# Storing gK and gV from ScalarE's queue, two steps late, in the stage that runs the second pass alone

## The chip, the cores and the metric

The kernel runs on one core of one Trainium2 chip. A core has five engines that each work through a queue of their own in order: TensorE (PE; its weight loads are shown as PEld), VectorE (DVE), ScalarE (ACT), GpSimd (POOL) and SyncE (SP). All share 16 DMA engines, to which SP, ACT and POOL can issue transfers. The metric is the time of one execution on the device in microseconds; the kernel before takes 891.21 us (median of 3 runs, 891.13 to 893.05).

## What is computed

The reference is one decoder layer in decode (2 batches, one token, width 640, 32 heads of 128, a cache of 4096 positions for each head, a two-layer MLP), and its gradients for seven inputs:

```python
q = (x @ wq).reshape(B, Sq, Hq, Dh) ...
scores = jnp.einsum("bhqd,bhkd->bhqk", q, k) * (Dh ** -0.5)
p = _softmax(scores, axis=-1)
o = jnp.einsum("bhqk,bhkd->bhqd", p, v)
...
h = x + _A_ref(_layernorm(x, axis=-1), A_k_cache, A_v_cache, A_wq, A_wo)
h2 = h + _B_ref(_layernorm(h, axis=-1), B_w1, B_w2)
...
_out, _vjp = jax.vjp(_f, A_x, A_k_cache, A_v_cache, A_wq, A_wo, B_w1, B_w2)
```

Nearly all bytes belong to the caches. K and V are read (64 tiles of 1 MB each, one for each batch and head), and their gradients gK and gV are written (again 64 tiles of 1 MB each). For one head, with one query row, both gradients are outer products: gV is the softmax column times a row of the output's gradient, gK is the gradient of the scores times the row q.

## The kernel before

**Two passes.** The first pass (`p1_iter`, one call for a head) reads K and V and computes the scores, the softmax weights P, the attention's output and what the projections need. The second pass (`p2_iter(j)`, one call for a head) needs the gradient of the attention's output, which is known once the layer has been run forward and back as far as there. It reads V again (tile Wt; the last six heads of each batch were kept on the chip), and writes gK and gV. `plan` (lines 1157 to 1168) lists the iterations: first pass alone, then a stage where every second iteration of the first pass is joined by one of the second, then the second pass alone, which begins at its iteration 14 of 64 and at about 470 us. The change touches this last stage.

**One iteration of the second pass** is a generator with six steps; the main loop (lines 1267 to 1274) runs one step, then whatever load is due (`pump`), then a bit of the background work: the weight gradients (TensorE's o_ps, line 980, ScalarE's casts to ot, line 986, and their stores from ScalarE's queue, line 989), the gradient of x (VectorE's gxj at line 678) and the output projections' gradients. In iteration j:

- Four groups of transposes of Wt on TensorE (line 424, into two PSUM banks t_ps), each copied by ScalarE to t_sb (line 429) and then multiplied with the gradient row into dp (line 437).
- At the head of the iteration the last product of the iteration before is finished (`last_dp`), and VectorE makes the score gradient gsp from it (line 858). The broadcast of two rows for j goes through PSUM (line 877) into rb, by ScalarE (line 882); GpSimd makes pp, a copy of P (line 884).
- VectorE makes gK of iteration j - 1 in two halves (line 844), the first at the head, the second in step 2. At the end of step 2 it is stored (line 899) and its buffer given back.
- VectorE makes gV of iteration j in two halves, in steps 5 and 6. Up to iteration 32 of this stage the last eight of its 32 blocks are made by ScalarE (line 930). At the end of step 6 it is stored (line 931) and its buffer given back.

**What sets the order.** The order of the instructions on each engine is the order in which the program writes them; the engines meet by semaphores that are placed for every tile. Buffers of 1 MB are handed out by `take` and `give`, which keep lists by purpose: "ld" for loads, "g" for gK and gV, "f" for ot, "q" for weights. A buffer that was given back can be taken at once in the program; on the chip its next writer then waits until the store has landed. In the stage with the second pass alone "g" begins with five buffers and gets more as other tiles fall free (lines 1227 to 1238). All loads are issued from SP's queue (line 445 for K, V and W, line 1066 for wqs), the stores of gK and gV from GpSimd's (lines 899, 909, 931, 941), those of ot from ScalarE's.

The functions that the change touches:

Of the kernel before, what the change touches and what calls it, by code (L numbers as in the profile page):

```python
# [15 lines left out]
def kernel(  # L16
# [20 lines left out]
    nc = tc.nc  # L37
# [402 lines left out]
    def natural(cache, b, h):  # L440
        return cache[b, h].rearrange("(p sc) d -> p sc d", sc=NSC)
# [412 lines left out]
    def score_grad(j, c):  # L854
# [5 lines left out]
            in1=P_bf[:, b * H + h, :, None].to_broadcast([128, NSC, 2]), op0=ALU.add, op1=ALU.mult)  # L860
        return gsp

    def p2_iter(j, busy, act=0, own_gK=False, early=False):

        c = S2[j] if j < NP1 else None
        p = S2.get(j - 1)
        if p is not None:
            bp, hp = turns[j - 1]
            last_dp(j - 1, p)
            gsp = score_grad(j - 1, p)  # L870
        if c is not None:
            b, h = turns[j]
            go = gom[:, h, b, :, :]

            bank = pst([128, 512], FP32, "sps", "dp_ps")
            for k, col in enumerate((goc, qsc)):
                nc.tensor.matmul(bank[:, 128 + k * 128:256 + k * 128],  # L877
                                 lhsT=col[:, h, b:b + 1].to_broadcast([128, 128]), rhs=ident_bf[:],
                                 start=True, stop=True)
            c["dp"] = bank[:, 0:NSC]  # L880
            rb = mats.tile([128, 256], BF16, tag="rb", bufs=3, name="rb")
            nc.scalar.activation(out=rb[:], in_=bank[:, 128:384], func=ACT.Copy, scale=rt[:, b, h:h + 1])  # L882
            pp = small.tile([128, NSC, 2], BF16, tag="pp", bufs=2, name="pp")
            nc.gpsimd.tensor_copy(out=pp[:], in_=P_bf[:, b * H + h, :, None].to_broadcast([128, NSC, 2]))
            c.update(rb=rb, pp=pp)
            if act:
                pa = small.tile([128, 8], FP32, tag="pa", bufs=2, name="pa")
                nc.gpsimd.tensor_copy(out=pa[:], in_=P_bf[:, b * H + h, NSC - act:NSC])
            c["T0"] = pair_transpose(c["W"], 0, busy=busy)
        if p is not None:  # L890
            gK = take("g", [128, NSC, 128], "gK")
            outer_half(gK, p["rb"][:, 128:256], gsp, 0)
        yield
        if early:
            gV = take("g", [128, NSC, 128], "gV")
            outer_half(gV, c["rb"][:, 0:128], c["pp"], 0)
        if p is not None:
            outer_half(gK, p["rb"][:, 128:256], gsp, 1)
            nc.gpsimd.dma_start(out=natural(out_2, bp, hp), in_=gK[:])  # L899
            give(gK)  # L900
            del S2[j - 1]
        yield
        if c is None:
            return
        c["T1"] = pair_transpose(c["W"], 1, busy=busy)
        pair_matvec(c["dp"], c.pop("T0"), 0, go)
        if early:
            outer_half(gV, c["rb"][:, 0:128], c["pp"], 1)
            nc.gpsimd.dma_start(out=natural(out_3, b, h), in_=gV[:])
        yield  # L910
        c["T2"] = pair_transpose(c["W"], 2, busy=busy)
        pair_matvec(c["dp"], c.pop("T1"), 1, go)
        yield
        c["T3"] = pair_transpose(c["W"], 3, busy=busy)
        give(c["W"], "g" if j < H and j != 1 and owned["g"] < 3 else None)
        pair_matvec(c["dp"], c.pop("T2"), 2, go)
        if early:
            give(gV)
            yield
            last_dp(j, c)  # L920
            gsp = score_grad(j, c)
        else:
            gV = take("g", [128, NSC, 128], "gV")
            outer_half(gV, c["rb"][:, 0:128], c["pp"], 0)
            yield
            if own_gK:
                last_dp(j, c)
            outer_half(gV, c["rb"][:, 0:128], c["pp"], 1, act)
            for k in range(act):
                nc.scalar.activation(out=gV[:, NSC - act + k, :], in_=c["rb"][:, 0:128], func=ACT.Copy, scale=pa[:, k:k + 1])  # L930
            nc.gpsimd.dma_start(out=natural(out_3, b, h), in_=gV[:])  # L931
            give(gV)
            if own_gK:
                gsp = score_grad(j, c)
            yield
        if own_gK:
            gK = take("g", [128, NSC, 128], "gK")
            outer_half(gK, c["rb"][:, 128:256], gsp, 0)
            yield
            outer_half(gK, c["rb"][:, 128:256], gsp, 1)  # L940
            nc.gpsimd.dma_start(out=natural(out_2, b, h), in_=gK[:])
            give(gK)
            del S2[j]
            yield

# [267 lines left out]
    def p2_step():  # L1213
        nonlocal g2
        try:
            next(g2)
        except StopIteration:
            g2 = None

    for n, (i, j) in enumerate(plan):  # L1220
        all_go = all(("go", B - 1, h) in done for h in range(H))
        if i is None and plan[n - 1][0] is not None:
            pkp.release()
            big1 = tc.alloc_tile_pool(name="big1", bufs=1)
            for _ in range(2):
                more_home("ld", big1)
            share(ld=KEPT[1] + 4, g=5)
        if all_go and not late[0]:
            wop.release()
            big3 = tc.alloc_tile_pool(name="big3", bufs=1, side="right")  # L1230
            for tag in ("ld", "g", "g", "q", "q", "q"):
                more_home(tag, big3)
        late[0] = all_go
        more = int(late[0])
        if fin is not None and not bg2 and not bg3:
            share(ld=8 + 3 * more, g=7 + 3 * more)
        elif fin is not None and j >= H + KEPT[1] - 1:
            share(ld=5 + more, g=6 + 2 * more, f=3, q=2 + 3 * more)
        if j is not None:
            while g2 is not None:  # L1240
                p2_step()
            if j < NP1:
                bg_until(("go", *turns[j]))
            g2 = p2_iter(j, 0, 8 if i is None and j <= H else 0, i is not None and plan[n + 1][1] is None, j < EARLY)
        if i is None and ("w1", 1) in done and fin is None:
            wts.release()
            fin = tc.alloc_tile_pool(name="fin", bufs=1)
            big2 = tc.alloc_tile_pool(name="big2", bufs=1)
            more_home("f", big2)
            banks.update(sps=[2, 3], o=[4, 5, 6])  # L1250
            bg2.append(("fin", fin_gen(fin)))
            bg3.append(("gx", gx_gen(fin)))
        if i == 12:
            bg.append(("ga", ga_gen()))
        if i == H + 2:
            banks["bc"].insert(0, banks["sps"].pop(0))
        elif i == P2_AT:
            banks["bc"].remove(7)
            banks["sps"].insert(0, banks["bc"][0])
            banks["bc"] = [7]  # L1260
        rate = RATES[0 if i is not None and i <= H + 1 else 1 if j is None and i < P2_AT else
                     2 if i is not None else 3 if j <= H else 4]
        if i is None:
            spread[0] = 2
            at_k[0] = 1
            k = 0
            while g2 is not None:
                p2_step()
                pump()
                slot[0] = int(k in ((1, 3, 5) if j <= H else (1, 4)))  # L1270
                k += 1
                bg_step(0, rate)
                bg_step(1, RATE2 * (0.4 if spreading[0] else 1.0))
                bg_step(2, RATE3)
            continue
        at = MIXED if j is not None else REST
        for k, _ in enumerate(p1_iter(i, i < H + 1, 0)):
            for _ in range(at.get(k, 0)):
                if g2 is not None:
                    p2_step()  # L1280
            if k == 5 and not H + 2 < i < P2_AT + 6:
                a_heads(i)
            pump()

            spread[0] = 1 if i < P2_AT else 2
            at_k[0] = k
            if i >= P2_AT:
                slot[0] = int(k == 6 or (k == 1 and j is not None))
            elif i > H + 1:
                slot[0] = {1: 2, 3: 1, 4: 1, 6: 1}.get(k, 0)  # L1290
            else:
                slot[0] = int(k in (1, 6))
            bg_step(0, rate)
            bg_step(1, 0.0)
        if i is not None and i in (H + 1, NP1 + 1):
            bg.append((f"m{i // H - 1}", middle_gen(i // H - 1)))
    forced[0] = True
    slot[0] = 99
    left = [q for q in (bg, bg3, bg2) if q]
# [38 lines left out]
```

## Time and profile before

| what | value |
|---|---|
| runs | 891.21 us median (891.13 to 893.05) |
| the profiled execution | 888.48 us, with a span of 886.3 us |
| busy in the span | PE 738.8 us, PEld 618.2, DVE 681.3, ACT 498.8, POOL 204.1 |
| DMA | 361.85 MB, 408 GB/s over the span |
| loads and SP's stores (q1) | 211.13 MB, 57.8% of the 16 engines' time |
| GpSimd's stores (q0) | 134.23 MB, 36.5% |
| ScalarE's stores (q10) | 14.92 MB, 4.1% |
| from issue to landing, median | gV 14.9 us, gK 15.0, Wt 11.6 |
| the chain that ended last | PE 35%, DMA 34%, DVE 16%, ACT 7%, issue 5% |

The profile is taken from one execution. Its span runs from the first to the last instruction of the program; 2.2 us of the execution lie around it. "Busy" counts instructions that compute; issues of DMAs count on GpSimd alone. The DMA share is the mean busy share of the 16 engines, which take packets from all queues. A wait is shown with what ended it: "DVE gV L844 <- DMA out_dram<-gK" is VectorE's operation at line 844 that writes gV, which waited until a store of gK had landed.

### The profile page before, as it was taken

How to read it: one execution, taken by the hardware profiler on the slowest of the kernel's cores; microseconds unless marked ns; L12 is line 12 of the kernel's file. 1: busy time of each engine (PE TensorE's matmuls, PEld its weight loads, DVE VectorE, ACT ScalarE, POOL GpSimd, SP SyncE). 2: the span in 40 equal slices, each digit the busy share in tenths (PEclk: the TensorE clock that was granted, in tenths of full speed). 3: DMA queues.
4: the chain of work that ended last, by engine and by line, in shares of the span. 5: the costliest groups of instructions: out<-in, count | busy, mean ns of one | idle time of the engine just before them, and what ended most of it. 6: DMA issues, size and time to landing. Idle time of an engine off the chain costs nothing.

```text
span 886.3 us, 24732 instructions
## 1 busy us (share of the span) xinstructions
PE 738.8 (83%) x10143; PEld 618.2 (70%) x10143; DVE 681.3 (77%) x1281; ACT 498.8 (56%) x1292; POOL 204.1 (23%) x358
## 2 busy tenths in 40 slices
PE   4999899999999997988868767787877899867690
PEld 4887788888887886877757656665656667564550
DVE  2666787877788896876778887878788689989861
ACT  1444343446776664654536767777656766545570
POOL 1344433343312010000011332222222111111220
PEclk9999999999999999998995655555566755555555
DMA  9999999999879999999999999999999999999996
GB/s 380 423 420 414 417 409 417 425 423 412 332 295 402 423 423 426 422 426 425 414 398 396 418 421 421 420 413 420 419 416 403 417 425 420 425 425 425 425 424 275
DMA packets 56289, 361.85 MB, mean 408 GB/s; under 512 B 5680, under 2 KB 11760, under 8 KB 15472
## 3 DMA queue, kind: packets, MB, share of 16 engines
q1 hardware_dynamic: 34520, 211.13, 57.8%
q0 software_dynamic: 18432, 134.23, 36.5%
q10 hardware_dynamic: 3224, 14.92, 4.1%
q8 instruction: 80, 1.31, 0.5%
q14 instruction: 33, 0.27, 0.1%
HBM read 211.11 MB, written 149.13 MB: 406 GB/s over the span
## 4 chain that ended last, share of the span: by engine, by line
PE 35%; DMA 34%; DVE 16%; ACT 7%; issue 5%; SPq 0%; POOL 0%; ACTq 0%; POOLq 0%; DVEq 0%
DMA Vt<-in_A_v_cache_dram 15%; PE t_ps L424 14%; DMA out_dram<-gK 11%; PE m_ps L460 9%; DVE gK L844 4%; DVE gV L844 4%; DMA out_dram<-gV 3%; ACT gV L930 3%; PE s_ps L437 3%; DMA wqs<-in_A_wq_dram 3%; DVE pk L470 2%; PE u_ps L498 2%; ACT t_sb L429 2%; PE dp_ps L437 2%; DVE gxj L678 2%
## 5 line engine op out<-in xcount | busy, mean ns | idle before, releaser
L429 ACT COPY t_sb<-t_ps 128x512 f32<-128x512 f32 x479 | 273.1, 587 | 192.4 <-PE t_ps L424 188.6
L437 PEld LDWEIGHTS <-t_sb 128*128 128x128 bf16 x4096 | 178.9, 102 | 63.8 <-ACT t_sb L429 36.2
L424 PE MATMUL t_ps<-ident_f,Wt 128*128 128x128 f32 x832 | 198.6, 389 | 0.9 <-ACT t_sb L429 0.9
L470 DVE TENSOR_TENSOR pk<-Kt,ep 128x2048 bf16<-128x2048 bf16 (+1 forms) x128 | 152.6, 1193 | 47.1 <-ACT ep L524 29.0
L460 PE MATMUL m_ps<-pk,Vt 128*128 128x129 bf16 x2048 | 172.0, 223 | 19.9 <-DMA Vt<-in_A_v_cache_dram 18.8
L844 DVE TENSOR_TENSOR gK<-rb,gsp 128x2048 bf16<-128x2048 bf16 x128 | 153.4, 1227 | 13.3 <-DMA out_dram<-gV 8.5
L460 PEld LDWEIGHTS <-Vt 128*128 128x128 bf16 x2048 | 125.6, 99 | 50.2 <-issue 28.4
L424 PEld LDWEIGHTS t_ps<-ident_f,Wt 128*128 128x128 f32 x832 | 138.2, 202 | 31.9 <-issue 25.2
L424 PE MATMUL t_ps<-ident_f,Kt 128*128 128x128 f32 x1024 | 156.0, 286 | 2.5 <-DMA Kt<-in_A_k_cache_dram 1.9
L844 DVE TENSOR_TENSOR gV<-rb,pp 128x2048 bf16<-128x2048 bf16 (+1 forms) x128 | 142.7, 1139 | 16.3 <-DMA out_dram<-gK 9.9
L486 POOL COPY pk<-ep 128x16 bf16<-128x16 bf16 x80 | 83.6, 1046 | 158.4 <-ACT ep L524 80.0
L424 PEld LDWEIGHTS t_ps<-ident_f,Kt 128*128 128x128 f32 x1024 | 113.9, 145 | 5.0 <-ACT t_sb L429 2.7
L437 PE MATMUL dp_ps<-gom,t_sb 128*128 128x2 bf16 x2048 | 96.0, 168 | 25.1 <-ACT t_sb L429 24.7
L931 POOL DMA_DIRECT2D out_dram<-gV x62 | 33.0, 533 | 305.3 <-DVE gsp L858 135.1
L437 PE MATMUL s_ps<-qm,t_sb 128*128 128x2 bf16 x2048 | 87.4, 164 | 1.5 <-DVE t_sb L427 1.5
L986 ACT CAST ot<-o_ps 128x512 bf16<-128x512 f32 (+3 forms) x152 | 67.5, 491 | 8.4 <-DMA out_dram<-ot 5.2
L588 ACT CAST MT<-m_ps 128x128 bf16<-128x128 f32 x64 | 17.0, 266 | 94.5 <-PE m_ps L460 94.4
L899 POOL DMA_DIRECT2D out_dram<-gK x53 | 28.2, 533 | 135.4 <-DVE gK L844 104.9
L882 ACT ACTIVATE rb<-dp_ps,rt 128x256 bf16<-128x256 f32 x64 | 30.2, 472 | 44.7 <-PE dp_ps L877 43.4
L678 DVE CUSTOM_DVE_ANT_0 hbc<-wo_t,hbc 128x640 bf16<-128x640 bf16 x64 | 52.8, 825 | 0.3
L678 DVE CUSTOM_DVE_ANT_0 gxj<-wqs,gqr 128x1024 bf16<-128x1024 bf16 x40 | 48.7, 1217 | 1.0 <-DMA wqs<-in_A_wq_dram 0.8
L930 ACT ACTIVATE gV<-rb,pa 128x128 bf16<-128x128 bf16 x152 | 46.5, 392 | 3.9 <-DMA out_dram<-gK 3.9
(205 smaller groups left out, 758.2 us busy)
## 6 DMA issues: line engine op xcount, KB each, us to landing
Kt<-in_A_k_cache_dram SPq DMA_DIRECT2D x64, 1024.0 KB, 19.4
Vt<-in_A_v_cache_dram SPq DMA_DIRECT2D x64, 1024.0 KB, 15.5
out_dram<-gV POOLq DMA_DIRECT2D x64, 1024.0 KB, 14.9
out_dram<-gK POOLq DMA_DIRECT2D x64, 1024.0 KB, 15.0
Wt<-in_A_v_cache_dram SPq DMA_DIRECT2D x52, 1024.0 KB, 11.6
wq_t<-in_A_wq_dram SPq DMA_DIRECT2D x5, 1024.0 KB, 7.8
wo_t<-in_A_wo_dram SPq DMA_DIRECT2D x4, 1280.0 KB, 17.6
wqs<-in_A_wq_dram SPq DMA_DIRECT2D x5, 1024.0 KB, 22.3
```

Of the source, the lines that this page charges most:

```text
L424: nc.tensor.transpose(t_ps[:, j, :], natf[:, 2 * cc:2 * cc + 2, :].rearrange("p c k -> p (c k)"), ident_f[:])
L429: nc.scalar.copy(out=t_sb[:], in_=t_ps[:])
L437: nc.tensor.matmul(dst[:, sc:sc + 2], lhsT=v[:, j, :, par], rhs=vecs[:, par, :], start=(par == 0), stop=(par == 1))
L460: nc.tensor.matmul(r["m"][:, 0:129], lhsT=r["V"][:, sc, :], rhs=r["pk"][sc // HALF][:, sc % HALF, 0:129], start=(sc == 0), stop=(sc == NSC ...
L470: nc.vector.tensor_tensor(out=p["pk"][k][:, 0:n, 0:128].rearrange("p s (a two) -> p s a two", two=2), in0=p["K"][:, sl, :].rearrange("p s ...
L486: nc.gpsimd.tensor_copy(out=col, in_=e)
L678: nc.vector.tensor_tensor_reduce(out=junk[0:kc, 0:width], in0=in0, in1=in1, scale=1.0, scalar=0.0, op0=ALU.mult, op1=ALU.add, accum_out=acc)
L844: nc.vector.tensor_tensor(out=pairs_view(dst[:, sl, :]), in0=row.rearrange("p (a two) -> p a two", two=2)[:, None, :, :].to_broadcast([128 ...
L882: nc.scalar.activation(out=rb[:], in_=bank[:, 128:384], func=ACT.Copy, scale=rt[:, b, h:h + 1])
L930: nc.scalar.activation(out=gV[:, NSC - act + k, :], in_=c["rb"][:, 0:128], func=ACT.Copy, scale=pa[:, k:k + 1])
L931: nc.gpsimd.dma_start(out=natural(out_3, b, h), in_=gV[:])
L986: nc.scalar.copy(out=ot[0:P, k, n0:n0 + nn], in_=o_ps[0:P, 0:nn])
```

## The change

Two helpers, `store` and `send`, take the place of the four stores and of the `give` calls behind them. Before the stage in which the second pass runs alone, `store` does as before: it issues from GpSimd and gives the buffer back. In that stage it only notes the tile. `send` is called after every step of the second pass; a noted tile is stored from ScalarE's queue, and its buffer given back, in the second step after the one that completed it. What is left after the last iteration is sent at once.

```diff
+    unsent = []
+    alone = [False]
+    LAG = 2
+
+    def store(out_ap, t):
+
+        if alone[0]:
+            unsent.append([LAG, out_ap, t])
+        else:
+            nc.gpsimd.dma_start(out=out_ap, in_=t[:])
+            give(t)
+
+    def send(all_of_them=False):
+
+        for entry in list(unsent):
+            entry[0] -= 1
+            if entry[0] < 0 or all_of_them:
+                nc.scalar.dma_start(out=entry[1], in_=entry[2][:])
+                give(entry[2])
+                unsent.remove(entry)
+
...
             outer_half(gK, p["rb"][:, 128:256], gsp, 1)
-            nc.gpsimd.dma_start(out=natural(out_2, bp, hp), in_=gK[:])
-            give(gK)
+            store(natural(out_2, bp, hp), gK)
...
-            nc.gpsimd.dma_start(out=natural(out_3, b, h), in_=gV[:])
-            give(gV)
+            store(natural(out_3, b, h), gV)
...
         except StopIteration:
             g2 = None
+        send()
...
         if i is None:
+            alone[0] = True
             spread[0] = 2
...
+    send(True)
     forced[0] = True
```

The stores at lines 909 and 941 are changed in the same way. On ScalarE the store of gV then stands behind the first of the four transpose copies of the next iteration, and the store of gK behind the third.

More of the change, by code (lines that the diff above doesn't have):

```diff
@@ L930, in p2_iter @@
                 nc.scalar.activation(out=gV[:, NSC - act + k, :], in_=c["rb"][:, 0:128], func=ACT.Copy, scale=pa[:, k:k + 1])
-            nc.gpsimd.dma_start(out=natural(out_3, b, h), in_=gV[:])
-            give(gV)
+            store(natural(out_3, b, h), gV)
             if own_gK:
@@ L940, in p2_iter @@
             outer_half(gK, c["rb"][:, 128:256], gsp, 1)
-            nc.gpsimd.dma_start(out=natural(out_2, b, h), in_=gK[:])
-            give(gK)
+            store(natural(out_2, b, h), gK)
             del S2[j]
```

## The prediction

> **What bounds the kernel now.** I read, in this order: the page's DMA parts (2, 3, 6), a table of windows over the stage in which only the second pass runs (about 470 to 870 us), the waits, and the timeline at two places of that stage and at the end.
>
> ```profile
> 480.00:540.00 60.00, 44.15 (x513) 38.74 (x511) 51.17 (x90) 44.39 (x118) 20.15 (x36) 0.56 1.01 414
> 540.00:620.00 80.00, 62.65 (x585) 49.94 (x583) 64.26 (x120) 60.65 (x166) 19.79 (x37) 0.52 1.01 418
> 620.00:700.00 80.00, 64.15 (x721) 52.40 (x720) 65.33 (x105) 51.70 (x104) 17.77 (x33) 0.65 1.00 413
> 700.00:780.00 80.00, 73.51 (x606) 52.69 (x606) 70.23 (x98) 50.02 (x119) 11.98 (x25) 0.52 1.01 423
> 780.00:820.00 40.00, 27.86 (x237) 20.29 (x234) 35.42 (x47) 21.09 (x45) 5.61 (x12) 0.54 1.01 425
> 820.00:870.00 50.00, 37.22 (x302) 25.11 (x302) 36.43 (x50) 30.09 (x61) 10.38 (x21) 0.53 1.01 424
> 870.00:875.00 5.00, 0.00 (x0) 0.00 (x0) 0.00 (x0) 0.00 (x0) 0.23 (x1) 0.50 1.02 427
> 875.00:880.00 5.00, 0.00 (x0) 0.00 (x0) 0.00 (x0) 0.00 (x0) 0.00 (x0) 0.50 0.63 264
> 880.00:886.30 6.30, 0.00 (x0) 0.00 (x0) 0.00 (x0) 0.00 (x0) 0.00 (x0) 0.50 0.06 27
> ```
>
> The columns are the window, its length, the busy time of PE, PEld, DVE, ACT and POOL with their instructions, the granted clock, the DMA engines' share and GB/s. The share never falls below 1.00 from 480 to 875 us: the transfers set the end, and every compute engine has room (ACT 258 of 390 us busy, VectorE 323). The engines do not finish together. Adding 0.63 of 5.00 us and 0.06 of 6.30 us to 875 puts their mean end at 878.5 us, while GpSimd's drain at the end of the program, which outlasts the last store, runs from 869.7 us for 15.8 us, to 885.5. So the slowest engine is some 6 us behind the mean, and it sets the end.
>
> ```profile
> L931 POOL DMA_DIRECT2D out_dram<-gV x62: 531/533/533, 297.1 to 865.0; - x62
> L989 ACTq DMA_DIRECT2D out_dram<-ot x19: 338/343/703, 567.7 to 865.3; - x19
> DVE gV L844 <- DMA out_dram<-gK: 9.9, 11, 2.4
> DVE gK L844 <- DMA out_dram<-gV: 8.5, 7, 2.4
> ```
>
> The first two are min, median and max ns of one DMA issue from GpSimd and from ScalarE. The last two (total us, times, longest) show VectorE waiting for gradient buffers until their stores have landed: computing is held back by the transfers, as it must be where they are the bound.
>
> **The change, part by part.**
>
> *101 stores leave GpSimd.* In the built program 101 of the 128 gK and gV stores go (27 stay): 101 x 0.533 = 54 us of an engine that is 23% busy. Worth 0. The pp copy (line 884), which queues behind them, comes free earlier; no group that waits long waits for pp, so 0 again.
>
> *They enter ScalarE's queue:* 101 x 0.343 = 35 us of issue over 50 iterations of about 8 us (866.73 - 472.7 us, 49 steps between first and last score gradient), 0.69 us each. Bounds: 0, if an issue passes under the copy ahead of it, and 35 us, if each stands on ScalarE's path. The nearest rows:
>
> ```profile
> 860.85 0.59 ACT L429 COPY t_sb<-t_ps 128x512 f32<-128x512 f32 x1 [0.28 <-PE t_ps L424]
> ...
> 860.93 0.38 ACTq L989 DMA_DIRECT2D out_dram<-ot  x1
> ...
> 861.41 0.59 ACT L986 CAST ot<-o_ps 128x512 bf16<-128x512 f32 x1
> ```
>
> The issue runs inside the 0.59 us copy, and the cast starts as that copy ends (861.44). The new stores stand behind just such copies (gV behind the first transpose copy of the next iteration, gK behind its third), so I take 0. The cover is gone wherever a store has to wait.
>
> *They go out later.* One iteration near the end: gK is complete at 854.09 us and GpSimd issues at 854.38; ScalarE's third copy there ends at 856.46, 2.1 us later. gV is complete at 856.36, issued at 856.65; the next first copy ends at 861.44, 4.8 us later. Landing takes a median 15.7 us (gV), 16.3 (gK) and 11.1 (Wt) in this stage, so (15.7 + 16.3 + 0.8 x 11.1 + 0.4 x 11.7) / 8.0 = 5.7 transfers are under way on average; the delay takes at most 6.9 / 8.0 = 0.9 of them. Nearly five 1 MB transfers remain, 12 us of work at 424 GB/s. Worth 0. Buffers are also given back two steps later, but the transfers' pace, not the buffer, ends the waits shown above.
>
> *A wait for VectorE* is now in ScalarE's in-order queue; behind it stand the copies that feed TensorE's score gradient and the casts of ot. Until about 735 us, and from 825 us on, ScalarE reaches the store after VectorE is done (by 1 to 5 us at most places). Between, VectorE is later:
>
> ```profile
> 809.25 0.59 ACT L429 COPY t_sb<-t_ps 128x512 f32<-128x512 f32 x1 [0.71 <-PE t_ps L424]
> ...
> 811.03 0.59 ACT L429 COPY t_sb<-t_ps 128x512 f32<-128x512 f32 x1 [0.71 <-PE t_ps L424]
> ...
> 815.64 1.22 DVE L844 TENSOR_TENSOR gK<-rb,gsp 128x2048 bf16<-128x2048 bf16 x1
> ...
> 822.48 0.28 DVE L858 SCALAR_TENSOR_TENSOR gsp<-dp_ps,negdot,P_bf 128x64 bf16<-128x64 f32 x1
> ```
>
> The third copy ends at 809.84, gK at 816.86: a hold of 7.0 us, after which the fourth copy starts at 816.9 instead of 811.03. Its product (8 matmuls, 0.40 us) is there by 818, and VectorE asks for it at 822.48: 4.5 us to spare. The holds don't add up; the first takes away ScalarE's lead, the later ones find it in step. Bounds: 0, and 10 iterations x (7.0 - 4.5) = 25 us if the lead that is lost is missed each time. I take 0, since TensorE itself waits for VectorE there (4.17 us at 803.31).
>
> *Semaphores.* In the built program all DMAs of SP's and ScalarE's queues take eight semaphores in turn, and each waits until the one eight places earlier has landed; GpSimd's had eight of their own. With 5.7 under way the limit is idle. From about 735 to 815 us stores take up to 36 to 38 us and Wt up to 29 to land, with 9.6 us an iteration (seven gK tiles begun from 735.86 to 803.32 us): (36 + 38 + 29) / 9.6 = 11 under way. There the eight bind, SP's loads included, but with eight queued (19 us of work) no engine is empty, and the last Wt, issued at 811.0 us, is first read at 859.7. Worth 0.
>
> *The queues' shares.* Loads meet one queue of stores instead of two, and ot's stores stand behind gK and gV. The same bytes pass; 0.
>
> *The end.* The final gK is complete at 869.40; its issue costs 0.34 us instead of 0.53. The slowest engine is busy until about 884.5 in any case. 0.
>
> Sum: 886.3 us of span + 0; with the 2.2 us around it (888.48 - 886.3) the profiled execution would stay at 888.5. The median of the runs shown, 891.21, is 2.7 us above that one. Forecast: **891 us**, no change.
>
> **The rivals.**
>
> *Faster: the stores that GpSimd issues are themselves what makes the slow engine slow.* For it: the stage's rate is 413 to 418 GB/s at full share until 700 us, against 424 later; 220 us x 9 / 424 = 4.7 us. And the slowest engine's 6 us behind the mean. Against it: after 780 us the same stores run at 424 to 425, and nothing shows that one queue's packets are the cause. If half to all of one of these went: 3 to 6 us, 885 to 888, centre 886.5. Beside this stands the Trainium skill, page "DMA: Bandwidth & Descriptors", section "Latency and other measured facts": two of the engines (7 and 15) are usually slower, with descriptor rings of GpSimd's DMAs as a best guess. By that rule the 6 us would go, and the median would be 885. The uneven end agrees with it; that it is those engines, the trace does not show. The Trainium skill, page "SBUF — State Buffer", section "SBUF: two separate sides", adds that VectorE can lock GpSimd out while it writes descriptors, and advises ScalarE's or SP's queue. By that rule DMA engines sit idle; the share of 1.00 to 1.01 and an issue of 531 to 542 ns throughout speak against it here.
>
> *Slower: ScalarE's holds between 735 and 825 us cost TensorE its lead.* TensorE is 92% busy from 700 to 780 (73.51 of 80) and can lose 6.5 us there; VectorE is 88% busy. If a hold leaves it idle for 1.5 us in each of ten iterations, computing is 15 us late. The end has cover: the last store is issued at 869.7, the quickest gK store lands in 6.8 us, the last landing is near 884.5, so 8 us of lateness are free. The rest counts: 7 us, 898. It decides from 0.8 us lost per iteration; at the upper bound of 25 us it gives 908. For it: TensorE, VectorE and the DMA are all near full there. Against it: 4.5 us to spare in the iteration shown.
>
> *It doesn't do what it says:* only if ScalarE always came after VectorE anyway, or if the semaphores kept stores back; both end in the forecast's number.
>
> **How the numbers follow.** A measurement here tells 0.2%, 1.8 us, from no change. No change (889.4 to 893.0): 0.38, the likeliest. Faster rival, 885 to 889: 0.30. Slower rival, 893 to 908, most of it below 899: 0.32. The range reaches from 884.5 to 899; it leaves out the far part of the slower case (about 0.1) and a little below. The likeliest case's own range is 889.4 to 893.
>
> **What would show it.** Right: share still 1.00 to 1.01 from 480 to 875, rates as above, GpSimd's issues gone, ScalarE waiting for VectorE in front of stores only from 735 to 825 us. The faster rival: 420 GB/s or more before 700 us, and the share from 875 us on falling in one step. The slower: a share below 0.97 in some window after 780 us, TensorE idle behind ScalarE from 735 on, the last gK store issued after 878 us. I am wrong altogether if ScalarE's issue lasts microseconds, or if it waits for landings outside that stretch.

## The result, and the profile after

The kernel after takes 894.27 us (median of 20 runs, 891.78 to 899.17), the kernel before 890.00 us (median of 20 runs beside them). The ratio of the means is 1.0061, with a 95% interval of 1.0045 to 1.0077: slower by some 5.4 us (the medians differ by 4.3), where no change was forecast. The profiled execution of after took 892.75 us with a span of 890.9 us, 4.6 us more than the span of before. One execution differs from the next by several microseconds (889.7 us median of before in one set, 885.7 to 895.0). The 20 of after lie in two groups, 11 from 891.8 to 894.4 us and 9 from 896.5 to 899.2; the profiled one is of the first, and no profile shows what the second adds. So the sizes of losses below go by the intervals of the timed runs, and the profiles, one of each kernel, say where time goes in that execution.

The windows of the kernel after, in the columns of the prediction's first table (window, length, PE, PEld, DVE, ACT, POOL, clock, DMA share, GB/s):

```profile
480.00:540.00 60.00, 46.62 (x512) 41.22 (x510) 50.62 (x92) 44.84 (x121) 6.48 (x17) 0.50 1.01 420
...
620.00:700.00 80.00, 65.54 (x716) 53.87 (x715) 65.15 (x103) 51.63 (x104) 2.60 (x11) 0.61 0.99 405
700.00:780.00 80.00, 58.78 (x494) 42.45 (x493) 60.33 (x83) 40.27 (x94) 5.98 (x7) 0.54 1.01 419
...
820.00:870.00 50.00, 44.67 (x339) 29.03 (x339) 38.67 (x54) 33.78 (x69) 3.15 (x6) 0.53 0.95 391
870.00:875.00 5.00, 4.57 (x35) 2.55 (x32) 3.01 (x4) 4.34 (x9) 0.00 (x0) 0.50 0.66 274
...
880.00:890.90 10.90, 0.00 (x0) 0.00 (x0) 1.93 (x2) 0.00 (x0) 0.00 (x0) 0.50 0.72 300
```

Between 700 and 780 us the share is still 1.01, but TensorE does 58.78 us of work where before did 73.51: computing loses its lead while the DMA engines stay as busy as they were. The loss shows at the end. From 820 us on the DMA engines run short of work (0.95, then 0.66), because TensorE and VectorE are still making the last tiles, which in before were complete by 870 us.

The start times of VectorE's score gradient (line 858, one for each head) show when the lead went: from 473 us up to the one at 707 us after lags before by at most 3 us; the next starts at 729.1 us instead of 716.3, 12.8 us late; the last at 879.2 instead of 866.7, 12.5 late. The two rows at the jump, first before, then after:

```profile
716.33 0.28 DVE L858 SCALAR_TENSOR_TENSOR gsp<-dp_ps,negdot,P_bf 128x64 bf16<-128x64 f32 x1 [4.18 <-PE dp_ps L437]
```

```profile
729.12 0.28 DVE L858 SCALAR_TENSOR_TENSOR gsp<-dp_ps,negdot,P_bf 128x64 bf16<-128x64 f32 x1 [14.02 <-PE dp_ps L437]
```

Most of the lag is this one event (it shrinks to 9.8 us by 830 us and grows by 2.7 after that). Three views show the event: ScalarE's timeline of after, VectorE's, and the chain that ended last (start, length, what):

```profile
711.29 0.58 ACT L429 COPY t_sb<-t_ps 128x512 f32<-128x512 f32 x1 [0.43 <-PE t_ps L424]
721.24 0.34 ACTq L880 DMA_DIRECT2D out_dram<-gV  x1
721.62 0.75 ACT L1003 CAST ot<-o_ps 128x512 bf16<-128x512 f32 x2 [9.74 <-DMA out_dram<-gK]
```

```profile
703.17 2.35 DVE L844 TENSOR_TENSOR gV<-rb,pp 128x2048 bf16<-128x2048 bf16 x2
```

```profile
697.40 23.77 DMA out_dram<-gK
721.62 0.59 ACT ot L1003
```

VectorE finished the gV that is stored here at 705.52 us, and ScalarE comes to its store at 711.87. Yet the store goes out at 721.24. What it waits for is the store of gK that was issued at 697.40 and lands at 721.17: in the built program that is the transfer eight places earlier in the rotation of SP's and ScalarE's DMAs, and both use one semaphore. Behind the waiting store ScalarE holds the casts of ot and the transposes' copies, and TensorE runs dry (10.5 us without a matmul before 722.26).

The Trainium skill, page "DMA: Bandwidth & Descriptors", section "Why a DMA increments its semaphore by 16 and not by 1", gives a reason why a program would wait so: with two DMAs in flight on one semaphore a wait for the first one's count can pass before that one has landed, so each transfer in flight wants a semaphore of its own. The rows above fit it (721.17 us the landing, 721.24 the issue); what a shared count would do without the wait, no run here shows.

Loads are held in the same way. The DMA queue's own waits in after (total us, times, longest):

```profile
SPq L445 <- DMA out_dram<-gV: 67.8, 17, 9.4
...
SPq L445 <- DMA out_dram<-gK: 22.6, 7, 7.9
SPq L364 <- DMA out_dram<-gK: 19.6, 1, 19.6
```

In before no load of SP waits for a store of gK or gV.

### The profile page after: what moved, and what is told of

Its sections match the earlier page's. It is cut to its first block, busy times and chain, and to the rows that moved or that the text cites. A ratio compares the mean times of both kernels' runs of the same rounds, so it can differ in the third digit from the quotient of the medians.

```text
span 890.9 us, 24695 instructions
## 1 busy us (share of the span) xinstructions
PE 740.1 (83%) x10143; PEld 618.8 (69%) x10143; DVE 680.9 (76%) x1281; ACT 498.5 (56%) x1292; POOL 149.4 (17%) x257
## 5 line engine op out<-in xcount | busy, mean ns | idle before, releaser
L905 POOL COPY pp<-P_bf 128x64 bf16<-128x64 bf16 x64 | 31.8, 496 | 337.2 <-DVE gV L844 328.2
L858 DVE SCALAR_TENSOR_TENSOR gsp<-dp_ps,negdot,P_bf 128x64 bf16<-128x64 f32 x64 | 18.0, 282 | 56.8 <-PE dp_ps L437 56.4
## 6 DMA issues: line engine op xcount, KB each, us to landing
out_dram<-gK ACTq DMA_DIRECT2D x51, 1024.0 KB, 14.3
out_dram<-gK POOLq DMA_DIRECT2D x13, 1024.0 KB, 10.4
```

## The experiments

Theories, as the expectations name them: **P**, the eight semaphores that SP's and ScalarE's transfers share, with an issuing engine that stands in order behind a landing; **V**, ScalarE's waits for VectorE; **I**, the issues' own time on ScalarE; later **G**, another rotation of the buffers, and **Q**, stores that move worse from ScalarE's queue. Each kernel was timed against before on the same chip; the table has the ratio with its 95% interval, and how late the last score gradient starts against the profile of before (866.7 us).

| run | ratio | 95% interval | last score gradient |
|---|---|---|---|
| after | 1.0061 | 1.0045 to 1.0077 | +12.5 us |
| early_part | 1.0070 | 1.0046 to 1.0094 | +4.6 |
| late_part | 1.0047 | 1.0021 to 1.0073 | +14.3 |
| only_gv | 1.0085 | 1.0055 to 1.0116 | +12.1 |
| lag5 | 1.0059 | 1.0037 to 1.0082 | +12.6 |
| give_alone | 1.0022 | 1.0004 to 1.0039 | +5.1 |
| queue_alone | 1.0040 | 1.0022 to 1.0058 | +12.4 |
| late_old | 1.0009 | 0.9993 to 1.0026 | +9.6 |
| delay_alone | 0.9990 | 0.9968 to 1.0011 | -0.6 |
| loads_gpsimd | 0.9984 | 0.9965 to 1.0002 | +6.3 |
| halves | 1.1057 | 1.1025 to 1.1088 | +103.1 |
| ot_gpsimd | 1.0001 | 0.9981 to 1.0020 | +6.0 |
| early_old | 1.0035 | 1.0014 to 1.0055 | +2.0 |
| sync_old | 1.0107 | 1.0076 to 1.0137 | +9.2 |
| ot_sync | 1.0014 | 0.9992 to 1.0037 | +8.8 |
| after_loads_gpsimd | 1.0011 | 0.9987 to 1.0035 | +7.7 |

### First set: where, which stores, how late

early_part and late_part split the stage, only_gv splits the stores, lag5 takes five steps instead of two:

```diff
-            alone[0] = True
+            alone[0] = j <= 42      # early_part; late_part: j > 42
...
-        if alone[0]:
+        if alone[0] and out_ap.tensor.name == out_3.tensor.name:      # only_gv
...
-    LAG = 2
+    LAG = 5      # lag5
```

> ScalarE stores gK and gV only in iterations 14 to 42 (to about 697 us), GpSimd after that. In the profile of the kernel after, the score gradients lag those of before by 1 to 3 us up to 710 us and by 12.8 us from 729 us on, all of it from one hold of ScalarE (711.87 to 721.24 us), whose store of gV waited for the semaphore of the gK store issued at 697.40 and landed at 721.17. Theory P (eight shared semaphores, and a ScalarE that stands in order behind the landing): no such hold here, lag below 4 us at the end, time within 1.5 us of before. Theory V (ScalarE waits for VectorE from 735 us on): the same as before too. Theory I (the issues' own time on ScalarE): 58 of 101 stores, so 58/101 of the 5.4 us loss, +3 us.

> GpSimd stores gK and gV up to iteration 42, ScalarE only from iteration 43 on (about 697 us). P: a hold of 5 to 10 us before a ScalarE store between 700 and 740 us, ended by a landing and not by VectorE, and the whole loss: 4 to 6 us slower than before. V: 4 to 6 us slower too, but the lag grows from 735 us on, in steps ended by VectorE. I: 43 of 101 stores, +2.3 us, the lag growing evenly.

> Only gV goes to ScalarE's queue two steps late; gK stays with GpSimd, issued at once. P: 2.6 places of the eight per iteration instead of 3.6, so the transfer eight places earlier is three iterations (some 27 us) back and has mostly landed: holds by landings below 3 us, within 1.5 us of before. V: half of the waits for VectorE stay, +2 to +3 us. I: half of the issues, +2.7 us.

> The kernel after with the stores five steps behind VectorE instead of two: VectorE is done before ScalarE comes to any store. P: the places rotate as before, a hold by a landing between 700 and 740 us stays, 3 to 7 us slower than the kernel before. V: no hold left, within 1.5 us of the kernel before. I: the same 5 us slower as the kernel after, lag growing evenly.

All four lost 0.5 to 0.9%. P had foretold the loss of late_part and lag5 (with holds by a landing of 4.8 and 9.2 us at about 717 us), and was wrong on early_part and only_gv. early_part has no hold at 711 us, its last score gradient is 4.6 us late, and still it loses all; late_part loses nearly as much though up to 697 us every store leaves GpSimd as in before. So something else is in all of them. lag5 tells less than was meant: five steps later the profile still shows ScalarE waiting for VectorE (4.2 us at one place, 3.7 at another, between 700 and 830 us), so it does not take V's waits away.

The built programs of late_part and of before first differ in iteration 0 of the second pass, in the buffer that gK takes. In before, iterations 0 and 1 issue gV's store at line 909 and give the buffer back two steps later; `store` gives it back at once. The section on the change says that `store` does as before until the last stage: for line 909 that is not so.

### Second set: the give alone, the queue alone

```diff
             outer_half(gV, c["rb"][:, 0:128], c["pp"], 1)
             nc.gpsimd.dma_start(out=natural(out_3, b, h), in_=gV[:])
+            give(gV)      # give_alone, on the kernel before
...
         if early:
-            give(gV)
             yield
```

queue_alone is the kernel after with these two gives put back where before has them; late_old adds `alone[0] = j > 42` to it, and delay_alone issues the late stores from `nc.gpsimd`.

> The kernel before with one edit that the change carries along: in iterations 0 and 1 of the second pass (at about 265 to 285 us) gV's buffer is given back when its store is issued instead of two steps later. From then on gK and gV take other buffers; nothing else differs. All four runs so far were 4 to 7 us slower than before, also those in which few or no stores differ before 700 us, so the holds after 700 us can't be the whole cause. Theory G (buffers): this edit alone costs 3 to 6 us, 893 to 895. Theory P (semaphores and ScalarE's holds): within 1.5 us of before. A third, N (scatter of the executions): within 1.5 us too.

> The kernel after with that give of iterations 0 and 1 put back where the kernel before has it; 101 stores still go from ScalarE's queue two steps late. G: the loss goes, within 1.5 us of before. P: it stays, 4 to 6 us slower, with a hold of ScalarE by a landing between 700 and 740 us.

> As the run that stores from ScalarE only from iteration 43 on, with the give of iterations 0 and 1 as in before: up to 697 us it is the program of before, instruction by instruction. G: within 1.5 us of before. P: 3 to 6 us slower, score gradients level with before up to 707 us and 5 to 13 us late from 730 us on.

> Old give in iterations 0 and 1; from the stage of the second pass alone the stores and the gives come two steps late as in after, but from GpSimd's queue. G: within 1.5 us of before. P: within 1.5 us of before, since GpSimd has semaphores of its own and nothing that matters stands behind its stores. If the delay itself costs (stores later, buffers given back later): 2 us or more slower.

Neither theory holds alone: the give costs 0.22%, the queue 0.40%, together the 0.61% of after, as closely as intervals of 0.2% to either side can say. The delay with its later gives costs nothing (-0.10%, interval through 0). late_old lost less than P expected (0.09%), with 9.6 us of lag at the end. The hold that P foretold for queue_alone is there, at the same store as in after:

```profile
716.00 0.75 ACT L1005 CAST ot<-o_ps 128x512 bf16<-128x512 f32 x2 [5.94 <-DMA out_dram<-gK]
```

How the give costs is seen on VectorE at 266 us, first before, then give_alone, where GpSimd had issued gV's store at 262.65 us:

```profile
265.33 0.28 DVE L858 SCALAR_TENSOR_TENSOR gsp<-dp_ps,negdot,P_bf 128x64 bf16<-128x64 f32 x1 [0.36 <-PE dp_ps L437]
265.65 1.23 DVE L844 TENSOR_TENSOR gK<-rb,gsp 128x2048 bf16<-128x2048 bf16 x1
```

```profile
266.00 0.28 DVE L858 SCALAR_TENSOR_TENSOR gsp<-dp_ps,negdot,P_bf 128x64 bf16<-128x64 f32 x1 [0.36 <-PE dp_ps L437]
269.47 1.23 DVE L844 TENSOR_TENSOR gK<-rb,gsp 128x2048 bf16<-128x2048 bf16 x1 [3.19 <-DMA out_dram<-gV]
```

gK takes the buffer that was just given back, and waits until it has landed, while another one was free. The first pass, still running, is behind it on VectorE, and few transfers are queued there to cover it: from 260 to 300 us the DMA share is 0.87 to 0.95 in the seven profiles with the new give. Those moved 336 to 374 GB/s in that window (mean 356), the ten with the old one 364 to 393 (mean 380): 24 GB/s x 40 us / 424 GB/s = 2.3 us of transfers late, before the stage that the change is about, which has no slack on the DMA to make it up. The two groups overlap, so this is an estimate of the size; the wait for gV's landing (1.8 to 3.2 us) is in all seven and in none of the ten.

### Third set: the semaphores set apart

All on queue_alone:

```diff
-        nc.sync.dma_start(out=t[:], ...)
+        (nc.gpsimd if alone[0] else nc.sync).dma_start(out=t[:], ...)      # loads_gpsimd: lines 364, 367, 445, 1083
...
-                nc.scalar.dma_start(out=entry[1], in_=entry[2][:])
+                for r in (slice(0, 64), slice(64, 128)):      # halves
+                    nc.scalar.dma_start(out=entry[1][r], in_=entry[2][r])
...
-            nc.scalar.dma_start(out=out_ap, in_=src)
+            (nc.gpsimd if alone[0] else nc.scalar).dma_start(out=out_ap, in_=src)      # ot_gpsimd: line 1006
```

early_old is queue_alone with `alone[0] = j <= 42`.

> Based on the run with the old give (all 101 stores from ScalarE, two steps late; 3.6 us slower than before). In the stage of the second pass alone its 49 loads go from GpSimd's queue, which has eight semaphores of its own, so ScalarE's stores share their eight only with ot. Every wait for VectorE, every issue on ScalarE and the delay stay. P (eight shared semaphores): the loss goes, within 1.5 us of before, no hold of ScalarE over 2 us by a landing. V, I, or Q (stores move worse from ScalarE's queue): it stays, 3 to 5 us slower.

> Same base; each of the 101 stores is issued as two transfers of 64 partitions (512 KB each, packets as before), so an iteration takes 5.6 places of the eight instead of 3.6 and the transfer eight places earlier is only 1.4 iterations (11 us) back, less than the 14 us a store takes to land. P: ScalarE is held by landings in most iterations, also before 700 us, and the time grows by 10 us or more over before. V and Q: as with whole stores, 3 to 5 us slower than before. I: twice the issues, 7 us slower.

> Same base; the 19 stores of ot go from GpSimd's queue in this stage: 3.2 places per iteration instead of 3.6, and ot no longer lands behind gK and gV. P: part of the loss goes, 1 to 3 us slower than before. V, I, Q: 3 to 5 us slower as ever.

> Old give; ScalarE stores only in iterations 14 to 42 (to about 697 us), GpSimd after that. If the parts add up, 3.6 us for all and 0.9 us for iterations from 43 on leave 2 to 3 us slower than before. P says where: no load is issued between 640 and 667 us, the next one (of w2) is held some 4 us longer by a landing of gK, and only 2 to 3 transfers are under way at 655 to 670 us where before has 4 to 5. V: within 1.5 us of before, since VectorE is never late before 735 us.

loads_gpsimd is the clearest: same stores from the same queue, same delay, but loads on other semaphores, and the loss is gone (-0.16%, interval to +0.02%). Its loads also stand in another engine's queue; before with its loads on GpSimd was not run, so what that alone is worth is not known. Its windows:

```profile
700.00:780.00 80.00, 67.40 (x548) 48.36 (x548) 69.36 (x96) 44.81 (x105) 13.94 (x23) 0.51 1.01 425
...
820.00:870.00 50.00, 45.83 (x341) 29.83 (x340) 35.09 (x48) 35.53 (x71) 2.82 (x7) 0.50 0.96 401
...
875.00:880.00 5.00, 0.00 (x0) 0.00 (x0) 0.75 (x1) 0.00 (x0) 0.00 (x0) 0.50 1.03 433
880.00:886.80 6.80, 0.00 (x0) 0.00 (x0) 0.00 (x0) 0.00 (x0) 0.00 (x0) 0.50 0.26 108
```

TensorE does 67.40 us of work from 700 to 780 us (73.51 in before, 58.78 in after), and the store held in after at 711.87 to 721.24 us goes out at once here, at 708.22. Q and I fall with it as causes of the loss: the stores do not move worse from ScalarE's queue, and their issues are all still there. V falls too: ScalarE's waits for VectorE between 700 and 830 us add up to 13.7 us here, 16.6 in queue_alone and 15.1 in after. One point of the expectation did not come true: ScalarE still stands idle from 778.6 to 785.3 us, at the end (4.6 us) for a landing of gV.

The lag at the end, 6.3 us, lies within the 8 us that the prediction found free. It is not what that hold left: 5.4 us of lag at 782 us are down to 1.9 at 830, and 4.4 come after that. Such a growth after 830 us (1.9 to 5.7 us) is in each of the ten kernels, halves apart, that store from ScalarE there, and not in the five that don't (-2.3 to +1.0). So these stores do cost ScalarE's order some microseconds at the end even with the loads on other semaphores; whether by issues or by waits, no run tells, and it is free only while the whole lag stays under 8.

ot_gpsimd, which frees 0.4 of 3.6 places an iteration, did better than "part": 1.0001. Yet the holds are still there. ScalarE's at the store of 711 us is as long as in queue_alone, and SP's loads of Wt wait 58.8 us for landings of gV (54.4 in queue_alone):

```profile
714.72 0.75 ACT L1006 CAST ot<-o_ps 128x512 bf16<-128x512 f32 x2 [6.23 <-DMA out_dram<-gK]
```

Its lag ends at 6.0 us, under the 8, and nothing is lost: what the holds leave here at the end is free. No run is clearly faster than before; loads_gpsimd is the nearest to it.

halves can't be read as a test of P. Issuing half the partitions changed more than the number of places. The issue from ScalarE (min, median, max ns of one), first in after, then in halves, and one window of halves:

```profile
L880 ACTq DMA_DIRECT2D out_dram<-gK x51: 338/338/1617, 471.4 to 882.0; - x51
L880 ACTq DMA_DIRECT2D out_dram<-gV x50: 338/338/1467, 475.4 to 878.3; - x50
```

```profile
L882 ACTq DMA_DIRECT2D out_dram<-gK x102: 472/1086/3010, 469.6 to 974.7; - x102
...
L882 ACTq DMA_DIRECT2D out_dram<-gV x100: 472/608/2290, 475.6 to 971.2; - x100
```

```profile
540.00:620.00 80.00, 47.67 (x434) 38.46 (x435) 47.38 (x90) 47.89 (x133) 8.61 (x16) 0.52 0.96 324
```

ScalarE issues for some 172 us (102 x 1.086 + 100 x 0.608) instead of 34, and at a share of 0.96 the engines move 324 GB/s instead of the 417 of queue_alone.

early_old shows that the queue costs before 697 us too (0.35%), where the prediction saw the limit idle. Its last score gradient is only 2.0 us late; what is late is the transfers. SP issues no load between 643 and 673 us: one of w2 waits, the last 18.2 us for a landing of gK, and goes out 5 us later than in before. Its one profile moved only 364 GB/s from 260 to 300 us already, where the others with the old give moved 372 to 393, so how much of the 0.35% arises at 640 to 680 us is not settled.

### Fourth set: what the places hold, and the sum

sync_old is queue_alone with `nc.sync` in `send`; ot_sync has `nc.sync` for ot in the last stage; after_loads_gpsimd is the kernel after (new give) with the loads on GpSimd.

> Old give; the 101 stores two steps late, but from SP's queue. They rotate through the same eight semaphores among the same transfers, and no store stands in ScalarE's order any more; loads now stand behind stores that wait for VectorE or for a landing. If the cost sits in ScalarE's holds: within 1.5 us of before, score gradients level with before past 716 us. If it sits in the places themselves, through loads held and a backlog capped at eight: 3 us or more slower.

> Old give, gK and gV from ScalarE's queue as in after; the 19 stores of ot from SP's queue in this stage. The places are as in the run with all from ScalarE, but ot no longer lands behind gK and gV in one queue. If moving ot to GpSimd helped by the places it freed: 3 to 4 us slower than before. If it helped since ot lands sooner: within 1.5 us of before.

> The kernel after, with the new give of iterations 0 and 1, and the 49 loads of the last stage from GpSimd's queue. If the loss of after is the sum of the give (2 us) and the shared places (3.6 us), the second part goes: 0.5 to 2.5 us slower than before, and the transfers are 2 us behind from 290 us on as in all runs with the new give.

With the stores on SP's queue nothing of them stands in ScalarE's order, the score gradients are level at 716 us (+1.0), and the kernel is slower than with ScalarE (1.0107). Now it is the loads that stand behind: its window, and SP's longest waits in that window:

```profile
700.00:780.00 80.00, 63.81 (x524) 45.19 (x524) 59.86 (x83) 43.87 (x103) 5.98 (x7) 0.52 0.91 360
```

```profile
SPq L881 <- DMA out_dram<-ot: 23.8, 2, 12.4
SPq L1085 <- DMA out_dram<-ot: 16.9, 1, 16.9
```

So the hold on ScalarE is not needed for a loss; here the queue of SP, waiting for a place in the rotation, holds what is behind it. ot_sync (1.0014, 1.2 us) lies in the range of its second expectation, ot landing sooner, but its interval (-0.08 to +0.37%) reaches into the first, and in its profile ScalarE is held for 9.7 us at the store of 711 us: whether moving ot helped by the places or by its order among the stores stays open. after_loads_gpsimd fits the sum: without the second cause 0.11% are left, with an interval (-0.13 to +0.35%) that holds the give's 0.22% and 0 as well.

## Why the prediction was wrong

The forecast was 891 us, no change. The 894.27 us lie in the stated range, but only because that range took in most of the slower rival; none of it is owed to the forecast's own working. The rival "slower" had the right end, and its mechanism in part.

**101 stores leave GpSimd: worth 0.** Right; so is that pp is not missed.

**ScalarE's issue: 0, bounds 0 and 35 us.** Right up to 649 us: the issues last 338 ns as taken, and the score gradients lag by 1.2 us at 473 us and by 1.2 at 649, where 23 iterations of 0.69 us would have added 16. After 830 us some lag arises wherever ScalarE stores (see loads_gpsimd); the share of the issues in it is not known.

**They go out later: 0.** Right by delay_alone. But the step spoke only of the stage after 470 us. That the change also moves a give forward by two steps in iterations 0 and 1 is in no step: a missing term, +2 us (0.22%).

**A wait for VectorE: 0, from 735 to 825 us.** The size is right as far as loads_gpsimd shows, where these waits stay and no time is lost. That ScalarE would wait for nothing else before its stores was not: at 711.87 us VectorE was long done, as the step says for that time, and the store waited for a landing.

**Semaphores: "There the eight bind, SP's loads included, but with eight queued (19 us of work) no engine is empty ... Worth 0".** This is the step that failed. It found the limit, the stretch (735 to 815 us; it began at 711) and the 11 transfers that would want places. It asked only whether the DMA engines stay fed, and they do (share 1.01 from 700 to 820 us). It did not ask who stands behind the transfer that waits, as the step on VectorE had. The 11 transfers under way in that stretch of before are the lead that computing builds for the end. That backlog is gone in after: for the gK stores issued from 735 to 815 us the median from issue to landing is 35.0 us in before, 17.5 in after and 26.6 in loads_gpsimd. Whether the cap of eight drained it or the hold at 711 us that came before, no run parts. A second part of the step fails as well: "with 5.7 under way the limit is idle" takes a mean, where loads are held singly (one of w2 goes out at 671.8 us, 4 us later than in before). By the timed runs this part is not the smaller: early_old loses 0.35%, late_old, which has the hold at 711 us, 0.09%. The rates from 620 to 700 us do not settle it: 401 GB/s in queue_alone against 413 in before, but 412 in early_part, whose stores go the same way there.

**The end: "8 us of lateness are free, the rest counts".** Right for the queue's cost, and the most useful number of the prediction. Where only the lag at the end is late, the loss is near the lag less 8: queue_alone 12.4 - 8 = 4.4 us (0.40% are 3.6), late_old 1.6 (0.8), ot_sync 0.8 (1.2), ot_gpsimd and loads_gpsimd at 6.0 and 6.3 us lose nothing. After itself: the last gK store goes out at 881.96 us instead of 869.7, 12.3 - 8 = 4.3, and its span is 4.6 longer. That match is in part luck, since queue_alone has the same lag without the give; one profile does not part the two causes, the timed runs do. In other runs the rule does not give the loss: early_part and early_old lose 6.2 and 3.1 us at lags of 4.6 and 2.0, sync_old 9.5 at 9.2, give_alone 2.0 at 5.1. There the transfers are late for themselves. The bytes moved up to 820 us, against before's and at 424 GB/s, tell by how much: 0.2 us or less in late_old, ot_gpsimd and ot_sync, 2.0 in queue_alone, 2.6 to 4.7 in early_part, early_old and give_alone, 12.6 in sync_old. In 11 of the 16 profiles the span is longer than before's by the larger of this and of the lag less 8, to within 1 us; the other five miss by 2.0 to 3.4 (an observation made after the result).

**The queues' shares: 0.** Right: loads_gpsimd.

**The rivals.** Slower: the price of a lost lead was right, the cause not; not VectorE between 735 and 825 us, but a landing at 721. Two of its signs came (a share of 0.95 after 820 us, the last gK store at 881.96), but a share under 0.97 does not tell a loss: loads_gpsimd has 0.96 and ot_gpsimd 0.93 from 820 to 870 us. The sign of being "wrong altogether", ScalarE waiting for a landing outside 735 to 825 us, came true at 711. Faster: 420 GB/s came before 540 us, but 405 from 620 to 700. The slow engines of the Trainium skill's page were to give 885 us. No run shows those 6 us: in queue_alone and ot_sync GpSimd issues nothing after about 470 us, and neither is faster than before. As their other losses hide a gain, the rule itself is not settled; in loads_gpsimd, where they are gone, at most 3 us may have been gained (interval from -0.35%), though its loads are GpSimd's then. "Doesn't do what it says" named the semaphores as what could hold stores back, and put its price at none.

**What stays open.** only_gv (1.0085) takes fewer places than queue_alone with the give, and loses no less, with hardly a hold of ScalarE (the longest by a landing of gK or gV is 0.9 us) and one of a load (w2's, 10.4 us). In its profile most of the lag comes from one wait of VectorE, 8.6 us to 729.7 us, for a wqs load issued at 702.8; in before that load is issued at 697.8 and read at 717.8 without a wait. So a loss of this size can arise without ScalarE being held, and no run tells how. The parts of the queue's 0.40% before and after 697 us (0.35 and 0.09%) have intervals of about 0.2% to either side.

## What to carry to other kernels

Before a transfer is moved to another queue, look up in the built program which semaphore it will wait on and which transfers share it, and ask what stands in order behind the issue: a limit that starves no DMA engine can still stop the engine that issues, or hold the next load. A large number of transfers under way in a stage that is bound by them is a lead that the end lives on, so price a cap on it by how late the last tile comes, less the work still queued then. And when stores are moved into helpers, compare each give with the one it replaces, also in iterations that the change does not mean: a buffer given back earlier is taken earlier, with its store still landing.

## What the runs showed of the hardware that was not expected

A store of 64 partitions from ScalarE's queue is no half of one of 128. Its issue takes a median of 0.61 us (gV) and 1.09 us (gK) against 0.34, and from 540 to 620 us the rate falls from 417 (queue_alone) to 324 GB/s at a share of 0.96; with the 101 stores split in two the kernel takes 983.35 us instead of 893.36. Why was not tried.
